# The large low parts of two feed-forward weights in block 0: VectorE subtraction or adding DMA transfer

## The chip, the cores and the metric

The kernel runs on one core of one Trainium2 chip. The metric is the device time of a run in microseconds (us). The median of three runs of the kernel before is 1362.46 us.

## What is computed

The reference is a transformer-like block on one sequence of L = 2048 tokens with D = 576 channels. First comes a state-space convolution (S4D) with layer norm and modulation, then a feed-forward network with F = 4608 hidden units:

```python
x = A_u
mod = (_silu(c) @ w_mod).reshape(c.shape[0], 6, 1, -1)
sa, ca, ga, sb, cb, gb = (mod[:, 0], mod[:, 1], ...)
h = _layernorm(x) * (1 + ca) + sa
x = x + ga * _A_ref(h, ...)          # long convolution by FFT with a kernel made from A, C, dt
h = _layernorm(x) * (1 + cb) + sb
h = jnp.maximum(jnp.einsum("bsd,df->bsf", h, B_w1), 0)
x = x + gb * jnp.einsum("bsf,fd->bsd", h, B_w2)
```

## The kernel before

The 2048 tokens are cut into four blocks of 512. The convolution of block 0 is done ahead. Then the feed-forward network runs through `NB * NF` = 4 x 36 = 144 steps on TensorE; a step is 128 hidden units for the 512 tokens of one block. While the steps of a block run, a generator (`gens[b]`) supplies other work, which the method `step` in `ffn` doles out by a rate per block: in block 0 this is the rest of the convolution kernel (`KGen.rest`: loads of `W2r`, `W` and `Zr` from DRAM, VectorE rotations in lines 464 to 470, matmuls in line 498) and the whole convolution of block 1 (`conv(1)`: loads `Ua`, `Ka`, `R`, VectorE products in lines 1009 to 1015).

A number in float32 is split in two parts that TensorE multiplies in the form fp32r: a high part, which is the number rounded to fp32r, and a low part, which is the number minus its high part. Products of high with high, high with low and low with high are summed. So each step has 14 matmuls of 512 columns for `hps` (line 1309) and 14 for `acc` (line 1335). The hidden units are split by ScalarE and VectorE (`hh`, line 1314, and `hl`, line 1315).

The weights are split in block 0 as they come in, and the low parts are kept in DRAM for blocks 1 to 3. In step g of block 0:

- SyncE (SP) loads `r1` (128 x 640, line 1254, for step g + 3) and `r2` (128 x 576, line 1258, for step g + 2). There are two buffers of each, so that a load waits until the last reader of the buffer two steps back is done.
- ScalarE (ACT) makes the high parts: `hi1`, line 1274 (128 x 640), and `hi2`, line 1284 (128 x 576).
- VectorE (DVE) makes the low parts: `lo1`, line 1279 (128 x 640), and `lo2`, lines 1290 (128 x 64) and 1291 (128 x 512).
- SP writes the low parts to DRAM (`L1d`, `L2d`, line 1390), out of the list `late`, one step after they were made. The weight buffers `w1` and `w2` are three deep.

From block 1 on (g >= 36) the low parts are loaded from `L1d` and `L2d`, and there is no subtraction.

GpSimd (POOL) issues the loads of `KGen.rest` and of `conv` through the software queue (q0); SP's transfers go through the hardware queue (q1). The order on each engine comes from a scheduler, except where an instruction is wrapped in `Kept`, which keeps it in program order with the others so wrapped. For the first three steps the splitting is wrapped, and in the profile its rows stand under line 47, the line of `Kept`. An engine takes its instructions in order, so one that waits holds up all behind it.

Of the kernel before, what the change touches and what calls it, by code (L numbers as in the profile page):

```python
# [10 lines left out]
F32 = mybir.dt.float32  # L11
F32R = mybir.dt.float32r
I32 = mybir.dt.int32
AF = mybir.ActivationFunctionType
ALU = mybir.AluOpType
# [5 lines left out]
D = 576  # L21
# [3 lines left out]
NF = F // P  # L25
# [24 lines left out]
class KGen:  # L50
# [10 lines left out]
    def v(self, out, a, b, op):  # L61
        self.tc.keep_in_program_order(self.nc.vector.tensor_tensor(out, a, b, op=op))  # L62
# [488 lines left out]
class Body:  # L551
# [194 lines left out]
    def main(self, ctx, kg, hooks):  # L746
# [32 lines left out]
        with ExitStack() as c:  # L779
            self.cps = self.pool(c, "cps0", space=PSUM)  # L780
            self.tps = self.pool(c, "tps", space=PSUM)
            self.cv = self.pool(c, "cv0", side="right")
            self.cvl = self.pool(c, "cvl", side="right")
            self.nps, self.ns = 4, 6
            mods, ffn = self.mod_late(), self.ffn(gens)
            self.vec = Kept(tc, nc.vector)
            for w in self.conv(0):
                if w == "mod":
                    next(mods, None)
                elif w in ("weights", "high", "low"):  # L790
                    next(ffn)
                elif w == "rows":
                    hooks[w]()
                elif w in hooks:
                    for _ in hooks[w]:
                        pass
            self.vec = nc.vector
# [444 lines left out]
    def ffn(self, gens):  # L1242

        nc, I, ff = self.nc, self.I, self.ff
        n = NB * NF
        r1, r2, w1, w2 = {}, {}, {}, {}
# [20 lines left out]
        def vec(g):  # L1267
            return (Kept(self.tc, nc.vector) if g < 3 else nc.vector).tensor_tensor

        def copy(g):  # L1270
            return (Kept(self.tc, nc.scalar) if g < 3 else nc.scalar).activation

        def hi1(g):
            copy(g - 1)(w1[g][:, 0], r1[g], AF.Copy)  # L1274

        def lo1(g):
            w, r = w1[g], r1.pop(g)
            if g < NF:
                vec(g)(w[:, 1], r, w[:, 0], op=ALU.subtract)  # L1279
                late.append((self.L1d[g], w[:, 1].rearrange("p k c -> p (k c)")))  # L1280

        def hi2(g):
            w = w2[g] = ff.tile([P, 1152], F32R, tag="w2", bufs=3, name="w2")
            copy(g)(w[:, 0:D], r2[g], AF.Copy)  # L1284

        def lo2(g):
            w, r = w2[g], r2.pop(g)
            if g < NF:
                v = vec(g)
                v(w[:, D:640], r[:, 512:D], w[:, 512:D], op=ALU.subtract)  # L1290
                v(w[:, 640:], r[:, :512], w[:, :512], op=ALU.subtract)
                late.append((self.L2d[g], w[:, D:]))
            else:
                nc.sync.dma_start(out=w[:, D:].bitcast(F32), in_=self.L2d[g % NF])
# [77 lines left out]
        for f in (hi1, hi2):  # L1372
            f(0)
        hi1(1)
        yield
        lo1(0)
        lo2(0)
        lo1(1)
        yield
        load_r2(1)  # L1380
        load_r1(2)
        prev = None
        for g in range(n + 1):
            if g < n:
                if g + 3 < n:
                    load_r1(g + 3)
                if g + 2 < n:
                    load_r2(g + 2)
                for dst, src in late:
                    nc.sync.dma_start(out=dst, in_=src.bitcast(F32))  # L1390
                late.clear()
                new = (g, *first(g))
                if g + 1 < n:
                    hi2(g + 1)
                    lo2(g + 1)
                if g + 2 < n:
                    hi1(g + 2)
                    lo1(g + 2)
                if g + 3 < n:
                    low1(g + 3)  # L1400
                step(g)
            if prev is not None:
                second(*prev)
                if prev[0] % NF == NF - 1:
                    self.evacuate(prev[0] // NF)
            if g < n:
                prev = new
                step(g)
                if g % NF == NF - 1:
                    for _ in gens[g // NF]:  # L1410
                        pass
                    done[0] = 0.0
# [126 lines left out]
```

## Time and profile before

| | |
|---|---|
| median of 3 runs (lowest to highest) | 1362.46 us (1361.05 to 1364.14) |
| the profiled execution | 1357.89 us; its span 1356.1 us |
| mean granted TensorE clock | 0.944 |
| PE busy | 1239.6 us (91%), 10720 matmuls |
| VectorE busy | 891.6 us (66%), 1324 instructions |
| ScalarE busy | 494.9 us (36%), 863 instructions |
| GpSimd busy | 162.6 us (12%), 260 instructions |
| DMA | 345.85 MB, mean 255 GB/s |

Busy times are of the whole span. Block 0 of the feed-forward network runs from about 228 to about 568 us of the span; only there the weights are split. A group's row has the line, the engine, the operation, out<-in, the shapes and the count; behind the first bar stand the busy time in us and the mean duration of one in ns, behind the second the idle time of the engine before it and what ended it. `w` is a buffer of `w1` or `w2`, and `r` one of `r1` or `r2` (the profile leaves buffer numbers out).

### The profile page before, as it was taken

How to read it: one execution, taken by the hardware profiler on the slowest of the kernel's cores; microseconds unless marked ns; L12 is line 12 of the kernel's file. 1: busy time of each engine (PE TensorE's matmuls, PEld its weight loads, DVE VectorE, ACT ScalarE, POOL GpSimd, SP SyncE). 2: the span in 40 equal slices, each digit the busy share in tenths (PEclk: the TensorE clock that was granted, in tenths of full speed). 3: DMA queues.
4: the chain of work that ended last, by engine and by line, in shares of the span. 5: the costliest groups of instructions: out<-in, count | busy, mean ns of one | idle time of the engine just before them, and what ended most of it. 6: DMA issues, size and time to landing. Idle time of an engine off the chain costs nothing.

```text
span 1356.1 us, 26019 instructions
## 1 busy us (share of the span) xinstructions
PE 1239.6 (91%) x10720; PEld 986.5 (73%) x10720; DVE 891.6 (66%) x1324; ACT 494.9 (36%) x863; POOL 162.6 (12%) x260
## 2 busy tenths in 40 slices
PE   4566777899989999999999999999999999999997
PEld 2345555677767687777777887887888888888885
DVE  5889988999955899678556986367997222111112
ACT  5678423222122432622234225433322353233231
POOL 0657511000010100020000000100000000000000
PEclk9558887999978999999999999999999999999998
DMA  8557973776897877798778995777996557666651
GB/s 267 221 223 291 328 271 130 282 249 248 320 332 277 296 248 269 239 382 311 250 246 327 363 371 158 269 230 245 370 387 194 176 175 228 201 195 195 201 184 53
DMA packets 120843, 345.85 MB, mean 255 GB/s; under 512 B 23916, under 2 KB 24212, under 8 KB 109972
## 3 DMA queue, kind: packets, MB, share of 16 engines
q1 hardware_dynamic: 103828, 226.96, 49.7%
q0 software_dynamic: 16384, 115.85, 22.8%
q8 instruction: 84, 1.38, 0.4%
q10 hardware_dynamic: 512, 1.38, 0.3%
q14 instruction: 35, 0.29, 0.1%
HBM read 262.73 MB, written 81.40 MB: 254 GB/s over the span
## 4 chain that ended last, share of the span: by engine, by line
PE 73%; DVE 15%; DMA 5%; issue 4%; ACT 1%; POOL 1%; SPq 0%; ACTq 0%; DVEq 0%; POOLq 0%
PE acc L1335 29%; PE hps L1309 29%; PE kps L498 4%; PE ps_f L829 4%; PE kps L71 2%; PE ph L71 2%; PE ps_i L1036 2%; DVE T L464 1%; DVE W1r L466 1%; DVE T L62 1%; DMA Ua<-Ud 1%; DVE Y L1015 1%; DMA r<-in_w_dram 1%; DMA kd<-ker 1%; DVE W L62 1%
## 5 line engine op out<-in xcount | busy, mean ns | idle before, releaser
L1309 PE MATMUL hps<-xh,w 128*128 128x512 f32 x1152 | 391.3, 400 | 0.7 <-ACT xh L47 0.7
L1335 PE MATMUL acc<-w,hh 128*128 128x512 f32 x1152 | 371.8, 403 | 7.0 <-ACT hh L1314 7.0
L1315 DVE SCALAR_TENSOR_TENSOR hl<-hps,hh 128x512 fp32r<-128x512 f32 x144 | 99.0, 687 | 322.9 <-ACT hh L1314 321.9
L1335 PEld LDWEIGHTS acc<-w,hh 128*128 128x128 f32 x1152 | 217.6, 190 | 55.1 <-ACT hh L1314 8.3
L1309 PEld LDWEIGHTS hps<-xh,w 128*128 128x128 f32 x1152 | 217.3, 190 | 48.5 <-ACT xh L47 1.3
L1309 PE MATMUL hps<-xl,w 128*128 128x512 f32 x576 | 230.7, 401 | 0.2
L1335 PE MATMUL acc<-w,hl 128*128 128x512 f32 x576 | 224.4, 402 | 3.9 <-DVE hl L1315 3.9
L1314 ACT ACTIVATE hh<-hps 128x512 fp32r<-128x512 f32 x144 | 85.9, 597 | 304.0 <-PE hps L1309 302.3
L1284 ACT ACTIVATE w<-r 128x576 fp32r<-128x576 f32 x141 | 96.6, 685 | 236.7 <-PE acc L1335 207.9
L1335 PEld LDWEIGHTS acc<-w,hl 128*128 128x128 f32 x576 | 109.1, 190 | 28.2 <-DVE hl L1315 5.0
L1309 PEld LDWEIGHTS hps<-xl,w 128*128 128x128 f32 x576 | 108.7, 189 | 24.5 <-DVE xl L47 0.8
L1274 ACT ACTIVATE w<-r 128x640 fp32r<-128x640 f32 x140 | 102.6, 733 | 40.6 <-DMA r<-in_w_dram 40.6
L1309 PE MATMUL hps<-xs,w 128*128 128x512 f32 x288 | 97.1, 410 | 0.3 <-DVE w L1279 0.3
L498 PEld LDWEIGHTS kps<-W1r,W2r 128*32 128x32 f32 x3456 | 66.9, 146 | 32.0 <-issue 23.6
L498 PE MATMUL kps<-W1r,W2r 128*32 128x48 f32 (+2 forms) x3456 | 75.9, 238 | 9.2 <-issue 8.2
L71 PE MATMUL kps<-W,W 128*32 128x16 f32 x2304 | 45.1, 218 | 42.7 <-POOL W L68 28.7
L71 PEld LDWEIGHTS kps<-W,W 128*32 128x32 f32 x2304 | 40.4, 150 | 55.0 <-POOL W L68 30.7
L1015 DVE TENSOR_TENSOR Y<-Y,T 128x1152 f32<-128x1152 f32 x60 | 79.4, 1349 | 0.0
L830 ACT ACTIVATE Z<-ps_f 128x288 f32<-128x288 f32 x120 | 48.7, 408 | 68.8 <-PE ps_f L829 67.6
L1453 POOL DMA_DIRECT2D out_dram<-x x16 | 8.7, 544 | 469.0 <-DVE x L1445 466.3
L1309 PEld LDWEIGHTS hps<-xs,w 128*128 128x128 f32 x288 | 53.3, 188 | 12.4 <-DVE w L1279 0.7
L1335 PE MATMUL acc<-hl,w 128*128 128x512 f32 x144 | 57.3, 398 | 0.0
(230 smaller groups left out, 1567.3 us busy)
## 6 DMA issues: line engine op xcount, KB each, us to landing
r<-in_w_dram SPq DMA_DIRECT2D x144, 320.0 KB, 3.5
r<-in_w_dram SPq DMA_DIRECT2D x144, 288.0 KB, 3.7
w<-L1d SPq DMA_DIRECT2D x108, 320.0 KB
w<-L2d SPq DMA_DIRECT2D x108, 288.0 KB, 2.6
W2r<-W2d POOLq DMA_DIRECT2D x18, 1536.0 KB, 8.3
W2d<-W SPq DMA_DIRECT2D x12, 1536.0 KB, 8.6
Ua<-Ud POOLq DMA_DIRECT2D x15, 1152.0 KB, 9.4
W<-W1d POOLq DMA_DIRECT2D x18, 768.0 KB, 10.7
```

The lines of the kernel that those rows point to most:

```text
L62: self.tc.keep_in_program_order(self.nc.vector.tensor_tensor(out, a, b, op=op))
L71: self.tc.keep_in_program_order(self.nc.tensor.matmul(*args, **kw))
L498: nc.tensor.matmul(ps[32 * dd : 32 * dd + 32, q, :], W2[:, r, :, ch], W1[:, :, r, ch], start=(r == 0), stop=(r == 1),)
L829: nc.tensor.matmul(o, fc[:, n2, c, :], src(n2), start=True, stop=True)
L830: ev = nc.scalar.activation(Z[:, n2, c], ps[:, :PC], AF.Copy)
L1015: v(y, y, T, op=op or ALU.add)
L1274: copy(g - 1)(w1[g][:, 0], r1[g], AF.Copy)
L1284: copy(g)(w[:, 0:D], r2[g], AF.Copy)
L1309: nc.tensor.matmul(ps, a, x, start=(i == 0), stop=(i == 13))
L1314: nc.scalar.activation(hh, ps, AF.Relu)
L1315: nc.vector.scalar_tensor_tensor(hl, ps, 0.0, hh, op0=ALU.max, op1=ALU.subtract)
L1335: nc.tensor.matmul(acc[i], a, x, start=(f == 0 and seen[i] == 1), stop=(f == NF - 1 and seen[i] == (3 if i < 4 else 2)),)
```

## The change

In block 0, ScalarE now makes a second, negated copy of the rounded weight in the place of the low part, and a transfer issued by GpSimd adds the unrounded weight onto it: -high + r = low. This replaces the subtraction of 128 x 640 (`lo1`) and the one of 128 x 512 (`lo2`). The small subtraction of 128 x 64 stays on VectorE. The negated copy is the same copy with a scale of -1, and so the negated high part.

```diff
         def hi1(g):
             copy(g - 1)(w1[g][:, 0], r1[g], AF.Copy)
+            if g < NF:
+                copy(g - 1)(w1[g][:, 1], r1[g], AF.Copy, scale=-1.0)
 
         def lo1(g):
             w, r = w1[g], r1.pop(g)
             if g < NF:
-                vec(g)(w[:, 1], r, w[:, 0], op=ALU.subtract)
+                nc.gpsimd.dma_start(
+                    out=w[:, 1].rearrange("p k c -> p (k c)").bitcast(F32),
+                    in_=r.rearrange("p k c -> p (k c)"), accum_op=ALU.add,
+                )
                 late.append((self.L1d[g], w[:, 1].rearrange("p k c -> p (k c)")))
 
         def hi2(g):
             w = w2[g] = ff.tile([P, 1152], F32R, tag="w2", bufs=3, name="w2")
             copy(g)(w[:, 0:D], r2[g], AF.Copy)
+            if g < NF:
+                copy(g)(w[:, 640:], r2[g][:, :512], AF.Copy, scale=-1.0)
 
         def lo2(g):
             w, r = w2[g], r2.pop(g)
             if g < NF:
-                v = vec(g)
-                v(w[:, D:640], r[:, 512:D], w[:, 512:D], op=ALU.subtract)
-                v(w[:, 640:], r[:, :512], w[:, :512], op=ALU.subtract)
+                vec(g)(w[:, D:640], r[:, 512:D], w[:, 512:D], op=ALU.subtract)
+                nc.gpsimd.dma_start(
+                    out=w[:, 640:].bitcast(F32), in_=r[:, 0:512], accum_op=ALU.add
+                )
                 late.append((self.L2d[g], w[:, D:]))
```

The change shifts line numbers: the two adding transfers are lines 1281 and 1297, the negated copies 1276 and 1291, the high part of `w2` is line 1289, `hh` is 1322, the matmuls 1317 and 1343, and the writes to `L1d` and `L2d` line 1398.

The order of the instructions shows three places. The first is GpSimd's queue in the middle of block 0's kernel work (`W2r`, `W`, `Zr` are the loads of three successive pieces of it). Before:

```order
L47 DMA W2r_4_3733<-W2d_4_69 128x3072
L47 DMA W0_6_3735<-W1d_6_83 128x1536
L47 DMA Zr_6_3736<-Zd_6_95 128x192
L47 DMA W2r_5_3947<-W2d_5_70 128x3072
L47 DMA W0_7_3949<-W1d_7_84 128x1536
L47 DMA Zr_7_3950<-Zd_7_96 128x192
```

The same loads after the change:

```order
L47 DMA W2r_4_3754<-W2d_4_69 128x3072
L47 DMA W0_6_3756<-W1d_6_83 128x1536
L1297 DMA w2_3833<-r2_3695 128x512
L47 DMA Zr_6_3757<-Zd_6_95 128x192
L1281 DMA w1_3753<-r1_3693 128x640
L1281 DMA w1_3841<-r1_3807 128x640
L1297 DMA w2_3938<-r2_3809 128x512
L47 DMA W2r_5_3972<-W2d_5_70 128x3072
L47 DMA W0_7_3974<-W1d_7_84 128x1536
L47 DMA Zr_7_3975<-Zd_7_96 128x192
```

Four adding transfers, those of two steps, stand in the queue between one set of loads and the next.

The second is SP's queue at the same stage, with the semaphores that each waits for (DMASW: a transfer of GpSimd's queue has landed; DMAHW: one of SP's). Before:

```order
L1258 DMA r_3249<-in_w_dram 128x576 [waits DMAHW6_49,DVE_49,Activation_49]
L1254 DMA r_3247<-in_w_dram 128x640 [waits DMAHW7_49,DVE_49,Activation_49]
L1390 DMA L2d_167<-w_3195 128x576 [waits DMAHW0_49]
L1390 DMA L1d_132<-w_3098 128x640 [waits DMAHW1_49]
L1258 DMA r_3360<-in_w_dram 128x576 [waits DMAHW2_49,DVE_49,Activation_49]
```

After:

```order
L1254 DMA r_3589<-in_w_dram 128x640 [waits DMAHW2_49,DMAHW4_49,DMASW3_49,Activation_49]
L1398 DMA L1d_135<-w_3405 128x640 [waits DMAHW3_49]
L1258 DMA r_3591<-in_w_dram 128x576 [waits DMASW2_49,DVE_49]
L1398 DMA L2d_170<-w_3536 128x576 [waits DMAHW5_49]
L1254 DMA r_3693<-in_w_dram 128x640 [waits DMAHW6_49,DMASW0_49,Activation_49]
```

A load of a weight waited for VectorE's subtraction, and now waits for the landing of the adding transfer that reads the same buffer.

The third is ScalarE's queue, one step of the same stage. Before:

```order
L1284 ACTIVATE w2_3598<-r2_3463 128x576
L1274 ACTIVATE w1_3527<-r1_3461 128x640
L1314 ACTIVATE hh_3594<-hps_3578 128x512
L508 ACTIVATE ker_0_3115<-kps_3544 128x48x6
L1284 ACTIVATE w2_3726<-r2_3574 128x576
```

After:

```order
L1289 ACTIVATE w2_3397<-r2_3260 128x576
L1291 ACTIVATE w2_3397<-r2_3260 128x512
L1322 ACTIVATE hh_3393<-hps_3377 128x512
L508 ACTIVATE ker_0_3124<-kps_3343 128x48x6
L1289 ACTIVATE w2_3536<-r2_3373 128x576
L1291 ACTIVATE w2_3536<-r2_3373 128x512
L1274 ACTIVATE w1_3405<-r1_3371 128x640
```

Each copy of a weight has a second one behind it, ahead of the next `hh`.

## The prediction

> **What bounds the kernel now.** The change touches block 0 of the feed-forward network alone, so I read the busy times by stretch first: the kernel work (228 to 344 us), its end and the transforms of block 1 (344 to 460), the products of block 1 (460 to 568), all of block 0, and two stretches of later blocks. Behind the busy times stand the granted clock, the DMA share and GB/s.
>
> ```profile
> core 0: us, PE busy (x) PEld busy (x) DVE busy (x) ACT busy (x) POOL busy (x), PEclk, DMA share, GB/s
> 228.00:344.00 116.00, 109.02 (x1304) 85.48 (x1303) 115.27 (x120) 29.57 (x51) 11.48 (x22) 0.97 0.75 270
> 344.00:460.00 116.00, 106.95 (x1657) 83.24 (x1657) 79.06 (x120) 30.45 (x67) 11.48 (x20) 0.91 0.85 302
> 460.00:568.00 108.00, 105.12 (x456) 82.01 (x455) 94.80 (x151) 41.68 (x76) 4.24 (x8) 1.00 0.76 268
> 228.00:568.00 340.00, 321.08 (x3415) 250.73 (x3414) 289.13 (x389) 101.71 (x193) 27.20 (x49) 0.96 0.78 280
> ...
> 750.00:800.00 50.00, 50.00 (x220) 41.09 (x219) 44.57 (x53) 13.39 (x21) 4.25 (x8) 1.00 0.98 372
> ...
> 1200.00:1250.00 50.00, 50.00 (x223) 41.39 (x221) 5.53 (x8) 14.73 (x24) 0.00 (x0) 1.00 0.65 199
> ```
>
> In the first stretch VectorE is busy 115.27 of 116 us: it is the bound there. But the DMA engines are busy 0.75 to 0.85 of the time all through block 0; later they reach 0.98 with TensorE full.
>
> A busy TensorE isn't TensorE at its peak, so I work out its floor. In the last row above it has nothing else to do and runs a 512-column matmul each 50 / 223 = 0.224 us. The rows of the first stretch alone, by line (1309, 1335, then the kernel's 498):
>
> ```profile
> 228.00:344.00 116.00, 44.17 (x170) 30.67 (x168) 0.97 0.75 270
> ...
> 228.00:344.00 116.00, 46.98 (x174) 32.81 (x175) 0.97 0.75 270
> ...
> 228.00:344.00 116.00, 26.34 (x960) 22.39 (x960) 0.97 0.75 270
> ```
>
> 170 + 174 big ones make 77.1 us, with 26.3 us of line 498 the floor is 103.4 of 116 us. So VectorE costs at most 12.6 us here.
>
> The timeline of VectorE shows the same by step (start, duration; the `hl` of one step and that two steps on):
>
> ```profile
> 256.92 0.68 DVE L1315 SCALAR_TENSOR_TENSOR hl<-hps,hh 128x512 fp32r<-128x512 f32 x1
> ...
> 269.88 0.68 DVE L1291 TENSOR_TENSOR w<-r,w 128x512 fp32r<-128x512 f32 x1
> 270.48 0.81 DVE L1279 TENSOR_TENSOR w<-r,w 128x640 fp32r<-128x640 f32 x1
> 271.21 3.42 DVE L466 TENSOR_TENSOR W1r<-W,Zr 128x1536 f32<-128x1536 f32 x2
> ...
> 276.29 0.68 DVE L1315 SCALAR_TENSOR_TENSOR hl<-hps,hh 128x512 fp32r<-128x512 f32 x1
> ```
>
> Two steps take 276.29 - 256.92 = 19.37 us. From start to start the two subtractions that go take 0.60 and 0.73 us.
>
> Last the chain of waits, in whose block 0 stand waits for transfers too; its two longest (start, us):
>
> ```profile
> 280.17 11.73 DMA r<-in_w_dram
> ...
> 512.35 12.85 DMA Ua<-Ud
> ```
>
> One is a weight's load (`r`), the other a load of GpSimd's queue: both kinds get company from the change.
>
> **The change part by part.**
>
> *Removed from VectorE.* 0.60 + 0.73 = 1.33 us in each step. In the first stretch (first two rows) 11 x 0.73 + 10 x 0.60 = 14 us of VectorE's 115 go; it would need 101 us, and TensorE's floor of 103.4 is next. At most 12.6 us are won.
>
> ```profile
> L1279 DVE TENSOR_TENSOR w<-r,w 128x640 fp32r<-128x640 f32 x11 | 9.0, 814 | 0.0
> ...
> L1291 DVE TENSOR_TENSOR w<-r,w 128x512 fp32r<-128x512 f32 x10 | 6.8, 681 | 0.0
> ...
> L1279 DVE TENSOR_TENSOR w<-r,w 128x640 fp32r<-128x640 f32 x11 | 9.0, 815 | 0.0
> ...
> L1291 DVE TENSOR_TENSOR w<-r,w 128x512 fp32r<-128x512 f32 x12 | 8.2, 681 | 0.0
> ```
>
> In the second stretch VectorE is busy 79 of 116 us and isn't last: nothing. In the third (last two rows) it is busy 94.8 of 108 us, and the chain has the transfer of 12.85 us. 11 x 0.73 + 12 x 0.60 make 15 us; I take two thirds, 10 us, an estimate, for VectorE isn't last all the time. The relief is at most 12.6 + 10 = 22 us.
>
> *Added to ScalarE.* Two copies a step. The nearest row is the copy of the high part:
>
> ```profile
> L1274 ACT ACTIVATE w<-r 128x640 fp32r<-128x640 f32 x140 | 102.6, 733 | 40.6 <-DMA r<-in_w_dram 40.6
> ```
>
> At most 2 x 0.73 = 1.46 us a step (one of the two is shorter), some 50 us in block 0, where ScalarE is busy 102 of 340. The cover is its idle time. It isn't perfect: the copies stand ahead of `hh`, and `hh` starts the second half of a step. ScalarE already waits for `r` with `hh` behind it. Cost nothing; without cover 1.46 us a step, about what VectorE gives back.
>
> *Added to GpSimd.* Two issues a step. A plain issue takes 0.54 us by the first row, the dearest in block 0 1.18 by the second; so 37 to 80 us more on an engine busy 27 of 340. The issue time is hidden. The queue is not: an adding transfer waits for ScalarE's copy, and the next `W2r`, `W`, `Zr` stand behind it; the other way round it waits behind a `W2r` that waits for TensorE, or a `Zr` that waits for VectorE.
>
> ```profile
> L1453 POOL DMA_DIRECT2D out_dram<-x x16 | 8.7, 544 | 469.0 <-DVE x L1445 466.3 <-DVE x L1451 2.5
> ...
> L1232 POOL DMA_DIRECT2D kt<-kd x6 | 7.0, 1175 | 60.5 <-PE ps_f L829 58.4 <-DVE W1r L468 2.0
> ```
>
> *Added to the DMA engines: the term that decides.* 320 KB and 256 KB more in each step. The rate at full share is 280 / 0.78 = 359 GB/s (the row of all block 0), so one pass of the bytes takes 0.91 + 0.73 = 1.64 us of all 16 engines. The trace has no adding transfer. It can't take less than about one plain pass; it has to fetch `r` and the destination and write the destination, three movements for a plain transfer's two, so 1.5 passes if fetching and writing count alike, and two if fetching alone sets the pace. I take 1.5 and keep 1 and 2 as the ends. Some 35 steps' weights fall between 228 and 568. Now the engines are busy 0.78 x 340 = 265 us there; 35 x 1.64 = 57 us a pass makes 322, 351 or 380 us for 1, 1.5 or 2 passes. The window of 340 us doesn't hold 351. At 0.95, a little under the 0.98 that the row of 750 to 800 us reaches (block 0's own best stretch has 0.85), the three need 339, 369 and 400 us: no gain, +29, +60.
>
> A page speaks against the change here: the Trainium skill, *Collectives: The Full Stack*, section "The bandwidth ceiling: the fold count and why AG ≠ RS ≠ AR", holds that a reducing transfer runs at half the rate of a copying one, since both operands are fetched through the same reading side. By that rule it is two passes and +60; no run here shows it. Another speaks for it: *DMA: Bandwidth & Descriptors*, section "Where 436 GB/s comes from", gives SBUF to SBUF 435 GB/s where transfers with HBM have some 358. The 359 above agrees with the latter; by the former 1.5 passes would be an estimated 71 us instead of 86, and the sum about +14.
>
> *Moved: when a weight's buffer comes free.* A load of `r` waited for VectorE; now for the landing of the adding transfer, which goes into the same queue as the loads of the kernel work. Landings in the first stretch (count, KB, median us):
>
> ```profile
> W<-W1d POOLq DMA_DIRECT2D x8, 768.0 KB, 10.1
> r<-in_w_dram SPq DMA_DIRECT2D x12, 320.0 KB, 5.4
> ...
> Zr<-Zd POOLq DMA_DIRECT2D x8, 96.0 KB, 7.8
> ```
>
> `Zr` is small and takes 7.8 us because it stands behind `W2r` and `W`. A loop over two steps is then: adding transfer (some 8 to 10 us behind such a burst) + load 5.4 + four copies 2.9 + two issues about 1 = 17 to 19 us. VectorE without the subtractions needs 19.37 - 2.67 = 16.7. So the new loop is about as long as what it replaces, with nothing to spare. Queued behind the waiting load on SP are the other weight's load and both writes to `L1d` and `L2d`.
>
> *Sum.* VectorE's relief of up to 22 us is real but something else is last once it is gone: the DMA engines, at 369 us where block 0 takes 340. That is +29 us against the profiled execution's 1357.89, so about 1387; the median of the runs lies 4.6 above that execution, so 1391 on the median. About 0.2% (2.7 us) is what a measurement can tell from no change here.
>
> **The rivals.**
>
> *The relief pays (faster).* If the adding transfers take a pass or less and the share goes to 0.98 as it did at 750 us, block 0 needs 322 / 0.98 = 329 us: -11. With no loss at all it is -22. For it: the first stretch's VectorE at 99%, and idle DMA between bursts that an adding transfer could fill. It decides when the fetch of the destination costs nothing. 1340 to 1357, about 1351. Chance 0.20.
>
> *Even.* One pass at 0.95: 339 us for 340. 1360 to 1365. Chance 0.06.
>
> *Two passes.* 400 us, +60; with some of it in gaps +45 to +75: about 1422. For it: reading twice is the plain meaning of an add. Against: the 0.78 is a busy share that holds waits as well as bytes. Chance 0.20.
>
> *The buffer's loop.* If landings under the heavier load go to the longest that the chain shows (12.85 for a load of GpSimd's queue, 11.73 for `r`), the loop is 12.9 + 11.7 + 2.9 + 1 = 28.5 us for two steps, 9 over the 19.37, and 17 pairs give some +75 us whatever the bytes cost: about 1437. It decides once the two landings together exceed some 15.5 us. Against: most steps between bursts land sooner (the loads' median is 5.4). Chance 0.10.
>
> That the subtractions are not taken off VectorE is no rival: the order shows the adding transfers in their place.
>
> **How the numbers follow.** Forecast, more work on the DMA engines than block 0 has room for, +3 to +45: chance 0.44. Slower in all 0.44 + 0.20 + 0.10 = 0.74, same 0.06, faster 0.20. The range leaves out the better half of the faster case and the upper part of the two slowest cases, about 0.1 each: 1350 to 1428. The forecast's own range is 1365 to 1408.
>
> **What would show it.** Right: VectorE in block 0 down by some 45 us and no longer full in its first stretch; DMA share of block 0 at 0.9 or more; block 0 some 370 us long; loads of `r` and DMA waits longer in the chain, `hh` late behind a copy that waits for `r`; blocks 1 to 3 unchanged. Wrong: two steps of the first stretch at 17.5 us, near TensorE's floor, with a DMA share under 0.9 (the relief pays), or a step paced by one buffer's loop with a DMA share that hasn't risen.

## The result and the profile after

The kernel after takes 1409.45 us (median of 4 runs, 1401.38 to 1414.38) against 1362.7 us before: the ratio is 1.0338, with a 95% interval of 1.0287 to 1.0388. That is 46.8 us slower. The profiled execution took 1414.38 us with a span of 1412.6 us, at the upper end of its runs, so its loss of 56.5 us in the span is larger than that of the medians.

All of it arises in block 0. By the timeline, the `hl` of step 1 starts 0.9 us later than before, that of step 12 14.1 us later, of step 23 39.3 and of step 36 55.0; from step 40 on the distance is 56.6 to 56.7 us to the end.

The stretches of the kernel after, in the columns of the prediction's first table (block 0 is longer now, so the last row reaches to 615 us; a DMA packet counts whole in the stretch in which it starts, so a share can pass 1):

```profile
228.00:344.00 116.00, 99.74 (x1071) 77.07 (x1071) 92.14 (x89) 37.20 (x65) 30.19 (x42) 0.93 0.97 291
344.00:460.00 116.00, 93.95 (x1771) 75.14 (x1771) 51.88 (x71) 30.79 (x63) 25.22 (x34) 0.90 0.91 283
460.00:568.00 108.00, 96.81 (x365) 71.75 (x364) 71.55 (x105) 44.34 (x84) 25.65 (x34) 0.91 1.03 327
228.00:615.00 387.00, 331.14 (x3378) 255.39 (x3378) 245.84 (x320) 136.64 (x255) 88.73 (x119) 0.92 0.96 292
```

VectorE is no longer full in the first stretch (92.14 of 116 us) and is busy 246 us in block 0 instead of 289. The share of the DMA engines went from 0.78 to 0.96, and neither TensorE nor VectorE fills a stretch. The bound has moved to the DMA engines and to those who wait for them.

The DMA queues and issues of block 0, before (228 to 568 us) and then after (228 to 615 us): packets, MB and share of 16 engines; below, count, KB and median us to landing.

```profile
q1 hardware_dynamic: 21952, 48.44, 40.5%
q0 software_dynamic: 6176, 46.30, 37.3%
...
r<-in_w_dram SPq DMA_DIRECT2D x37, 320.0 KB, 5.2
...
r<-in_w_dram SPq DMA_DIRECT2D x37, 288.0 KB, 2.7
```

```profile
q0 software_dynamic: 16112, 66.62, 62.0%
q1 hardware_dynamic: 20800, 46.02, 33.4%
...
r<-in_w_dram SPq DMA_DIRECT2D x36, 320.0 KB, 4.8
w<-r POOLq DMA_DIRECT2D x34, 320.0 KB, 6.5
...
r<-in_w_dram SPq DMA_DIRECT2D x35, 288.0 KB, 6.7
...
w<-r POOLq DMA_DIRECT2D x35, 256.0 KB, 6.4
```

GpSimd's queue q0 was busy 0.373 x 340 = 127 us and is now busy 0.620 x 387 = 240 us: 113 us more of all 16 engines for 20.3 MB more, 5.57 us a MB. Before, it took 127 / 46.30 = 2.74 us a MB. An adding transfer thus costs 2.03 times what the same queue's plain ones cost per byte. The records of single packets say the same: a packet of 2560 bytes takes 215 ns (median) in an adding transfer and 102 ns in a load or write of SP, and the 69 adding transfers add up to 114 us of the 16 engines.

This alone sets a floor. The engines were busy 265 us in block 0 before; with 114 us more that is 379 us, and a share of 0.96 over the 396 us that block 0 takes in the profiled execution is 380. Even at a share of 1, 379 us are 39 more than the 340 of before, as long as the other transfers take what they took.

The chain of waits at the start of block 0 (start, us):

```profile
235.52 11.06 DMA w<-r
246.70 11.88 DMA r<-in_w_dram
...
270.90 12.51 DMA w<-r
283.47 5.62 DMA r<-in_w_dram
```

An adding transfer lands, and only then does the load into the buffer that it read start. SP's waits show the same. Before, the loads of lines 1254 and 1258 waited for VectorE; after, for the landing (us in total, times, longest):

```profile
SPq L1258 <- DVE w L1291: 169.1, 29, 13.0
...
SPq L1254 <- DVE w L1279: 34.6, 28, 7.6
```

```profile
SPq L1258 <- DMA w<-r: 160.6, 17, 39.8
SPq L1254 <- DMA w<-r: 134.5, 31, 18.1
```

The engines' waits after (us in total, times, longest): ScalarE waits for `r`, and VectorE's `hl` waits for ScalarE's `hh`, which stands behind those copies. `hl <- hh` was 20.8 us in 6 waits in block 0 before. GpSimd waits for the second copy, with the loads of the kernel work behind it.

```profile
POOL w L1297 <- ACT w L1291: 85.0, 15, 13.8
DVE hl L1323 <- ACT hh L1322: 71.6, 18, 11.9
POOL w L1281 <- ACT w L1276: 63.0, 14, 12.0
ACT w L1289 <- DMA r<-in_w_dram: 61.6, 15, 11.8
ACT w L1274 <- DMA r<-in_w_dram: 52.7, 16, 7.1
```

Two other ways to lose time are small in this trace. For loads of GpSimd's queue VectorE waited 18.2 us in all of block 0, and 13.0 us before (4.3 and 2.5 us of it for `Zr`). For an adding transfer to land TensorE waited 3.5 us at most.

So two readings are open. In the first (A), the DMA engines are full, and the bytes set the pace. In the second (B, with its kin C and E), latency does: the round from adding transfer to load to copy, through queues that work in order, whatever the bytes cost. The profile shows signs of both.

### The profile page after: what moved, and what is told of

Read it like the earlier page. It is cut to its first block, busy times and chain, and to the rows that moved or that the text cites. A ratio compares the mean times of both kernels' runs of the same rounds, so it can differ in the third digit from the quotient of the medians.

```text
span 1412.6 us, 26239 instructions
## 1 busy us (share of the span) xinstructions
PE 1258.2 (89%) x10720; PEld 997.7 (71%) x10720; DVE 847.7 (60%) x1252; ACT 535.4 (38%) x935; POOL 225.7 (16%) x332
## 4 chain that ended last, share of the span: by engine, by line
PE 67%; DMA 17%; DVE 6%; issue 5%; ACT 2%; POOL 1%; SPq 0%; POOLq 0%; ACTq 0%; DVEq 0%
PE acc L1343 27%; PE hps L1317 27%; DMA r<-in_w_dram 6%; DMA w<-r 6%; PE ps_f L829 4%; PE kps L498 3%; PE kps L71 2%; PE ph L71 2%; DMA L2d<-w 2%; PE ps_i L1036 2%; DVE T L62 1%; DMA Rd<-K 1%; PE ps_t L1131 1%; POOL W L68 1%; DMA kd<-ker 1%
## 5 line engine op out<-in xcount | busy, mean ns | idle before, releaser
L1343 PE MATMUL acc<-w,hh 128*128 128x512 f32 x1152 | 377.7, 405 | 3.5 <-ACT hh L1322 2.4
L1317 PE MATMUL hps<-xl,w 128*128 128x512 f32 x576 | 235.4, 409 | 0.7 <-DVE xl L47 0.5
L1343 PE MATMUL acc<-w,hl 128*128 128x512 f32 x576 | 232.2, 404 | 1.3 <-DVE hl L1323 1.3
L1343 PEld LDWEIGHTS acc<-w,hl 128*128 128x128 f32 x576 | 110.2, 191 | 25.9 <-DVE hl L1323 2.1
L1036 PE MATMUL ps_i<-V,gc 128*128 128x288 f32 x136 | 43.8, 458 | 19.2 <-DVE x L1041 11.3
```

The lines of the kernel that those rows point to most:

```text
L1036: nc.tensor.matmul(ps[:, :PC], a, b, start=(i == 0), stop=(i == len(ops) - 1))
L1317: nc.tensor.matmul(ps, a, x, start=(i == 0), stop=(i == 13))
L1343: nc.tensor.matmul(acc[i], a, x, start=(f == 0 and seen[i] == 1), stop=(f == NF - 1 and seen[i] == (3 if i < 4 else 2)),)
```

## The experiments

Each run is compared with the kernel before, run beside it on the same chip. Microseconds are differences of the medians.

| run | kernel it starts from | median us | against before | ratio (95% interval) |
|---|---|---|---|---|
| a_plain | after | 1378.22 | +19.2 | 1.0149 (1.0110 to 1.0188) |
| a_half | after | 1394.59 | +35.6 | 1.0257 (1.0231 to 1.0283) |
| a_tiny | after | 1370.97 | +11.9 | 1.0086 (1.0061 to 1.0112) |
| b_bytes | before | 1385.19 | +26.2 | 1.0192 (1.0171 to 1.0212) |
| a_free | after | 1413.03 | +53.0 | 1.0385 (1.0362 to 1.0409) |
| a_plainsp | a_plain | 1399.25 | +39.2 | 1.0285 (1.0251 to 1.0320) |
| b_bytes2 | before | 1361.65 | +1.6 | 1.0010 (0.9994 to 1.0025) |
| b_pool1 | before | 1384.94 | +24.9 | 1.0185 (1.0164 to 1.0206) |
| a_freeL0 | a_free | 1409.35 | +48.2 | 1.0360 (1.0329 to 1.0391) |
| a_L0 | after | 1425.82 | +64.7 | 1.0476 (1.0439 to 1.0514) |
| a_late | after | 1404.59 | +43.4 | 1.0319 (1.0280 to 1.0358) |
| b_part | before | 1369.75 | +10.7 | 1.0061 (1.0036 to 1.0086) |

The scheduler writes the order of the engines anew for each kernel. a_plain has the order of the kernel after on every engine, a_half and a_tiny have the same order as each other, and b_bytes and b_bytes2 have that of the kernel before except on GpSimd. In the others the interleaving moved too, and I read no meaning into differences of some 10 us between them.

**Fewer bytes: a_plain, a_half, a_tiny.** a_plain:

```diff
-                    in_=r.rearrange("p k c -> p (k c)"), accum_op=ALU.add,
+                    in_=r.rearrange("p k c -> p (k c)"),
...
-                    out=w[:, 640:].bitcast(F32), in_=r[:, 0:512], accum_op=ALU.add
+                    out=w[:, 640:].bitcast(F32), in_=r[:, 0:512]
```

> The kernel after, with both adding transfers turned into plain copies of the same tiles, so the low parts in block 0 hold the raw weight instead of the rounding rest (that part of the computation is wrong, nothing else). Issues, queues, copies and waits are the same; only the fetch of the destination goes. Theory A (the DMA engines are full, an adding transfer costs two passes of its bytes): one pass less, 57 us less of all 16 engines' time, so block 0 needs 322 us of transfers and the kernel comes to 1350 to 1370. Theory B (the loop of the two weight buffers through the landing, whatever the bytes cost): the landing stays behind the same bursts on the same queue, and the time stays at 1395 to 1410.

a_half, where the slices are cut to 320 and 256 columns, and a_tiny, where both are cut to 128:

```diff
-                    out=w[:, 1].rearrange("p k c -> p (k c)").bitcast(F32),
-                    in_=r.rearrange("p k c -> p (k c)"), accum_op=ALU.add,
+                    out=w[:, 1].rearrange("p k c -> p (k c)").bitcast(F32)[:, 0:320],
+                    in_=r.rearrange("p k c -> p (k c)")[:, 0:320], accum_op=ALU.add,
```

> The kernel after, with the adding transfers over half of the columns only (320 of 640 and 256 of 512); the other half of the low parts in block 0 keeps the negated high part (wrong there). Same issues, queues, copies and waits, half of the added bytes. Theory A: 57 us less of all 16 engines' time, as with the plain copy of all columns: 1350 to 1370, and the same as that run to about 5 us. Theory B: 1395 to 1410.

> The kernel after, with the adding transfers over 128 columns only (22% of the added bytes); the other columns of the low parts in block 0 keep the negated high part (wrong there). Same issues, queues, copies and waits. Theory A: 25 us of added transfer work fit into block 0, what VectorE gives back shows: 1342 to 1362, at or below the kernel before. Theory B, in its strong form (queue place and round trip, not bytes, set the pace): 1385 or more. The copies or the issues by themselves (ScalarE ahead of hh, GpSimd's order) would show here as a time above 1362 with a DMA share under 0.9.

By the packets' records the transfers in question cost 114 us of the 16 engines after, 64 in a_half, 52 in a_plain and 36 in a_tiny: small packets are dear (65 ns for 512 bytes, 121 for 1280, 215 for 2560). The losses stand in the same order: some 46, 36, 19 and 12 us. In the two pairs of equal order, 62 us less of transfer work (after to a_plain) saves some 27 us, and 27 us less (a_half to a_tiny) saves 24 us. So the size of the transfers counts, against B in its strong form. But a_plain, a_half and a_tiny should have been level with the kernel before by A (265 + 52 = 317, 265 + 64 = 329 and 265 + 36 = 301 us of work in a block 0 of 340 us), and they are not: a_plain and a_tiny lie between what A and B had expected, and a_half, at 1394.59 us, lies at B's lower end. The second stretch (344 to 460 us) of a_plain, a_half and a_tiny, in this order:

```profile
344.00:460.00 116.00, 103.42 (x1686) 81.62 (x1686) 55.34 (x82) 39.27 (x79) 21.05 (x37) 0.94 0.88 323
```

```profile
344.00:460.00 116.00, 90.31 (x1585) 72.67 (x1586) 47.99 (x70) 28.35 (x59) 23.99 (x33) 0.87 0.82 260
```

```profile
344.00:460.00 116.00, 103.27 (x1688) 81.70 (x1687) 57.33 (x82) 37.87 (x77) 28.47 (x38) 0.94 0.87 282
```

Here the engines have room (0.82 to 0.88), TensorE waits all the same, and a_half loses most with the lowest share: a loss that isn't full engines. Of its loss, 21.5 us arise between the `hl` of steps 12 and 14. The chain there (start, us):

```profile
334.13 11.15 DMA w<-r
...
347.55 12.58 DMA L2d<-w
360.17 0.61 ACT w L1291
```

An adding transfer landed late, and behind it a write held up ScalarE's next copy. a_tiny loses 7.6 us in these steps, so they make 13.9 of the 21.4 us that a_half loses more in the profiled executions. So the second pair says little on full engines; the first pair, with shares of 0.96 and 0.90 over block 0, is the better evidence. This also spoils the expectation that a_half and a_plain would be level; they are 16 us apart with 12 us between their transfer work. And a_tiny shows the sign that was named for the copies and issues by themselves, a time above 1362 with a share under 0.9 (1370.97 us; 0.87 from 228 to 615 us). No run has the copies and issues without any transfer, so how much of its 12 us they make is open.

**The bytes alone: b_bytes and b_bytes2.** b_bytes adds to the kernel before, in steps 3 to 12:

```diff
+        def more(g, i):
+            if 3 <= g < 13:
+                nc.gpsimd.dma_start(out=self.scr[:, i], in_=self.x2[0][:, i], accum_op=ALU.add)
```

> The kernel before, with the subtractions still on VectorE, and beside them adding transfers for which nobody waits: in steps 3 to 12 two a step of 576 columns x 128 rows each, from a tile in SBUF onto an idle scratch tile, 5.9 MB in all, the bytes of ten steps of the change. The output is that of the kernel before. Theory A: some 33 us of all 16 engines' time go into the first stretch, whose engines are busy 87 of 116 us; it overflows to 1368 to 1385. Theory B: no weight buffer waits for these landings, so 1360 to 1367.

This run missed its aim. The transfers waited for nothing that comes late, so the scheduler put 19 of the 20 ahead of the kernel work's first loads. GpSimd's timeline (start, duration, in brackets the idle time before it):

```profile
216.71 0.90 POOL L1277 DMA_DIRECT2D scr<-x  x1 [9.02 <-issue]
...
249.96 0.89 POOL L47 DMA_DIRECT2D W<-W1d  x1
```

The first load of `W` goes out at 249.96 us. By the starts of `hl`, the whole loss of the first stretch, 27.2 us, stands at step 1 and stays the same up to step 14. It shows what a queue in order can cost, and nothing on bytes. b_bytes2 reads the finished low part instead, and so takes its place in the right step:

```diff
+                more(g, w[:, 1].rearrange("p k c -> p (k c)")[:, 0:D], 0)
...
+                more(g, w[:, D:], 1)
```

> The kernel before, subtractions still on VectorE, and in steps 3 to 12 two adding transfers a step of 576 columns from the finished low part onto an idle scratch tile, issued on GpSimd's queue behind the subtraction (the earlier try issued them all at once ahead of the kernel work's first loads). Nobody but the next user of the scratch slot waits for them; output as before; the order on all engines but GpSimd is that of the kernel before. 20 transfers x 128 rows x about 0.195 us / 16 engines = 31 us of the engines' time in the first stretch, which has 87 of 116 us taken. Theory A: 118 us of transfers at a share of 0.95 make 124 us, 6 to 12 us slower. Theory B: no weight buffer waits, -2 to +3 us. If over 15 us, the order of GpSimd's queue (kernel work's loads behind transfers that wait for VectorE) is itself a cost.

```profile
228.00:344.00 116.00, 110.15 (x1307) 85.84 (x1308) 114.77 (x121) 29.16 (x49) 29.77 (x42) 1.00 0.98 304
```

The share in the first stretch is 0.98 and the time is that of before: +1.6 us, with 1 in the interval. By the starts of `hl` the distance is 2.0 us at step 0 and 2.0 at step 14. So 32 us of adding transfers (by their packets) took up nearly all of the 29 us that the first stretch had left, at no cost, with no weight's load waiting for them. That is no verdict against A, which becomes a cost only beyond that. It shows that a share of 0.98 over one stretch does no harm by itself; whether it would over all of block 0 was not tried.

**The waits: a_free, a_late, a_L0, a_freeL0.** a_free lets the transfer read the high part, so that `r` is free after ScalarE's copies:

```diff
-                    in_=r.rearrange("p k c -> p (k c)"), accum_op=ALU.add,
+                    in_=w[:, 0].rearrange("p k c -> p (k c)").bitcast(F32), accum_op=ALU.add,
...
-                    out=w[:, 640:].bitcast(F32), in_=r[:, 0:512], accum_op=ALU.add
+                    out=w[:, 640:].bitcast(F32), in_=w[:, 0:512].bitcast(F32), accum_op=ALU.add
```

> The kernel after, with the adding transfers fetching the high part (in the same weight tile) instead of the raw weight r, so that r is free after ScalarE's copies; the low parts in block 0 become zero (wrong there). Same bytes, same sizes of packets, same queue, and the products still wait for the landing; only the raw weight's buffer no longer waits for it. Theory A (full DMA engines): 114 us of added transfer work as in the kernel after, so the loss stays at 40 to 50 us. Theory B (loop of the raw weight's buffers): the loss falls to 20 us or less. If each carries half, some 30.

Nothing was gained. SP's waits in a_free name a reason that would save B:

```profile
SPq L1398 <- DMA w<-w: 134.1, 42, 9.3
```

The loads no longer wait for the landing, but the writes to `L1d` and `L2d` still do, in the same queue ahead of the loads. So theory E: SP's order holds the loads up. Three runs tested it.

a_late issues the writes one step later:

```diff
-                for dst, src in late:
+                for dst, src in late[:-2] if g < NF else late:
                     nc.sync.dma_start(out=dst, in_=src.bitcast(F32))
-                late.clear()
+                late = late[-2:] if g < NF else []
```

> The kernel after, with the writes to L1d and L2d of block 0 issued one step later, when the adding transfer should have landed; the output is that of the kernel after. Loads of r still wait for the landing. Theory A: 40 us slower or more than the kernel before. Theory E: as the run with the high part written, since the wait for r's buffer is left: 30 to 50 us; if the writes were what held SP, under 15 us, and a gain over the kernel after.

a_L0 writes the high part, and a_freeL0 does that and what a_free does, so that neither a load nor a write waits for a landing:

```diff
-                late.append((self.L1d[g], w[:, 1].rearrange("p k c -> p (k c)")))
+                late.append((self.L1d[g], w[:, 0].rearrange("p k c -> p (k c)")))
...
-                late.append((self.L2d[g], w[:, D:]))
+                late.append((self.L2d[g], w[:, 0:D]))
```

> The kernel after, with only the writes to L1d and L2d changed: they write the high part, ready with ScalarE's copy, and not the low part (wrong low parts in blocks 1 to 3). Loads of r still wait for the landing of the adding transfer that reads the same buffer. Same bytes. Theory A: 40 us slower or more. Theory E, if one of the two waits is enough to hold SP (the run that freed r alone gained nothing): 30 to 50 us slower. If the writes were what held SP: under 15 us.

> Both of SP's waits for the landing taken away, all bytes kept: the adding transfers fetch the high part instead of the raw weight (low parts in block 0 become zero), and the writes to L1d and L2d write the high part instead of the low part (wrong low parts in blocks 1 to 3), so that neither a load of r nor a write has to wait for a landing. Same adding transfers, same sizes, same GpSimd queue; the products still wait for the landing. Theory A (full DMA engines): the added 114 us stay, so 40 us slower or more than the kernel before. Theory E (SP's queue in order: loads of r stand behind something that waits for a landing, ScalarE's copies wait for r, hh and the products behind them): within 10 us of the kernel before on either side. Theory F (what is left is the product's own wait for the landing): 20 to 35 us slower.

a_late came out at 43 us, where both theories had it. a_L0 came out at 65, above E's 30 to 50; I have no reason for its being slower than the kernel after, except that its order differs. a_freeL0 is the telling one. Its row of block 0, SP's longest wait, and the loads:

```profile
228.00:615.00 387.00, 329.09 (x3393) 254.19 (x3393) 245.69 (x321) 139.11 (x260) 89.01 (x119) 0.92 0.95 295
```

```profile
SPq L1398 <- ACT w L1289: 159.2, 27, 14.6
```

```profile
r<-in_w_dram SPq DMA_DIRECT2D x36, 320.0 KB, 9.0
...
r<-in_w_dram SPq DMA_DIRECT2D x36, 288.0 KB, 9.8
```

No wait of SP for an adding transfer's landing is left; SP now waits for ScalarE, and ScalarE for the loads themselves, which take 9.0 and 9.8 us (medians) where they took 5.2 and 2.7. TensorE's own wait for the landings is 9.3 us at most (theory F had 20 to 35). The share is 0.95 and the loss 48 us. With the waits for landings gone and the bytes kept the loss is whole: E falls as the main cause, and A, with its floor of 39 us, stands. One reserve: SP's writes now stand in front of the loads and wait for ScalarE's copies, so a round through SP's queue is left in this run too, and no run has the bytes without any such round through all of block 0.

**The queue: a_plainsp.** a_plain's copies issued by SP:

```diff
-                nc.gpsimd.dma_start(
+                nc.sync.dma_start(
```

> The run with plain copies in place of the adding transfers (low parts of block 0 hold the raw weight, wrong there), now issued on SP's queue and not on GpSimd's. Same 52 us of added transfer work; they no longer stand behind the loads of the kernel work (W2r, W: 2.3 MB each time), but SP waits for ScalarE's copy ahead of the next loads. Theory A: as on GpSimd's queue, 14 to 25 us slower than the kernel before. Theory C, that the place in GpSimd's queue is what makes the landing late: a loss of 8 us or less.

Slower by 20 us than on GpSimd's queue: outside what C had (8 us or less), and outside what A had too (14 to 25). ScalarE's wait for `r` grew to 84.3 us, from 49.8 in a_plain: a copy that waits for ScalarE now stands in the queue of the loads. So the run brings a wait of its own and is no clean test of the place behind `W2r` and `W`; but with a share of 0.85 from 228 to 615 us it shows that 39 us can be lost without full engines.

**The relief: b_pool1 and b_part.** b_pool1 moves the first weight's subtraction to GpSimd, without a byte more:

```diff
-                vec(g)(w[:, 1], r, w[:, 0], op=ALU.subtract)
+                (Kept(self.tc, nc.gpsimd) if g < 3 else nc.gpsimd).tensor_tensor(w[:, 1], r, w[:, 0], op=ALU.subtract)
```

> The kernel before, with the first weight's subtraction (128x640) on GpSimd instead of VectorE; nothing else is changed, no bytes are added, the output is right. It asks whether VectorE's relief is worth anything in block 0. If VectorE bounds the first stretch (busy 115 of 116 us): 11 x 0.73 us there and some more in the third stretch, 5 to 12 us faster. If the next limit stands close (loads, TensorE), or GpSimd's subtraction comes late for its reader: same within 3 us or slower.

It gave no relief, and was 25 us slower. The groups of GpSimd and of VectorE in the first stretch of b_pool1, and the same line before:

```profile
L1279 POOL TENSOR_TENSOR w<-r,w 128x640 fp32r<-128x640 f32 x12 | 39.6, 3306 | 19.1 <-ACT w L1274 18.5 <-ACT w L47 0.5
```

```profile
L466 DVE TENSOR_TENSOR W1r<-W,Zr 128x1536 f32<-128x1536 f32 x12 | 24.7, 2093 | 0.0
```

```profile
L466 DVE TENSOR_TENSOR W1r<-W,Zr 128x1536 f32<-128x1536 f32 x12 | 20.5, 1749 | 0.0
```

The subtraction takes 3.31 us on GpSimd in this stretch, and VectorE's own instructions get longer beside it (1749 to 2093 ns); VectorE stays busy 114.78 of 116 us. So the run does not say what relief is worth.

b_part makes the change for the first weight of steps 4 to 12 alone, with the adding transfer of the kernel after:

```diff
+            if 4 <= g < 13:
+                copy(g - 1)(w1[g][:, 1], r1[g], AF.Copy, scale=-1.0)
...
+                if 4 <= g < 13:
+                    nc.gpsimd.dma_start(
+                        out=w[:, 1].rearrange("p k c -> p (k c)").bitcast(F32),
+                        in_=r.rearrange("p k c -> p (k c)"), accum_op=ALU.add,
+                    )
+                else:
+                    vec(g)(w[:, 1], r, w[:, 0], op=ALU.subtract)
```

> The kernel before, with the change made for the first weight of nine steps of the first stretch alone (steps 4 to 12; everything else is subtracted on VectorE as before; the output is right). Nine adding transfers of 320 KB take 9 x 1.79 us = 16 us of the DMA engines (60.9 us for 34 of them in the kernel after), so 103 of 116 us: they fit. VectorE gives back 9 x 0.73 = 6.6 us of 115. Theory A (only bytes beyond what the DMA engines have left cost time): up to 6 us faster by step 12, nothing lost later, so 2 to 6 us faster in all. If the longer way to the low part (ScalarE's copy, GpSimd's issue, the landing behind W2r and W) costs as much as VectorE gives back, as the run with 128 columns suggests: within 2 us, or up to 8 us slower.

It is 0.6% slower (1357.49 to 1374.2 us, a wide spread), where A had 2 to 6 us faster; its median, +10.7, lies above the other reading's "up to 8 us slower" as well. The profiled execution, at 1372.6 us, shows gain and loss apart. By the starts of `hl`, the distance to the kernel before goes from +5.3 us at step 4 to +2.2 at step 9: 0.62 us a step won, nearly the 0.73 that was taken off VectorE. Two jumps take it back, 5.5 us between steps 3 and 4 and 10.5 us between steps 9 and 10. At the first, ScalarE waits 10.3 us for an `r` whose load went out at 259.69 us, 0.35 us after a `W2r` of 1.5 MB. The second one in the chain, and on GpSimd's timeline:

```profile
323.55 11.72 DMA r<-in_w_dram
...
335.97 0.59 ACT hh L1322
```

```profile
323.39 0.54 POOL L47 DMA_DIRECT2D W2r<-W2d  x1 [5.78 <-PE kps L498]
323.92 0.54 POOL L47 DMA_DIRECT2D W<-W1d  x1
```

```profile
SPq L1254 <- DMA w<-r: 63.0, 8, 12.1
```

SP held the load of the first weight back until an adding transfer had landed. The load of the second weight, behind it in SP's queue, so went out at 323.55 us, in the same moment as 2.3 MB for the kernel work, and took 11.72 us; `hh` came 12 us later. The engines' share in this stretch is 0.87. This is what is left when the bytes fit: a load that meets a burst, the second time because a wait in SP's queue moved it there. I take it to be part of the 12 to 19 us of a_tiny and a_plain as well; the chain of a_tiny has the same pairs of landing and load, but it wasn't tested apart there.

No variant beat the kernel before.

## Why the prediction was right, and where its sizes were off

- **VectorE's relief.** Right in the busy time (289 to 246 us in block 0, "some 45 us"), and VectorE is no longer full in its first stretch. "At most 12.6" us there held as a bound: b_part wins 0.62 us a step for 0.73 taken off, five steps long. As a gain it was not reached: a_plain, with both subtractions gone, wins 4.1 us between steps 2 and 11, where 12.6 us over the twelve steps of the stretch would be 9.5 over these nine.
- **ScalarE's copies at nothing.** Their time is as predicted (725 and 617 ns). b_part, with one of the two copies, keeps most of VectorE's relief while they run, so that one costs little; that they stand ahead of `hh` shows in `hl`, which waits 71.6 us for it, because a copy ahead of it waits for `r`. A run with the copies alone is missing.
- **GpSimd's issue.** 0.86 and 0.88 us, between the two rows taken (0.54 and 1.18), and hidden. Of the two fears for its queue, the one for the loads that stand behind the adding transfers came true in a small part (18.2 us of VectorE's waits for them, 13.0 before). The other, that the transfers land late behind `W2r` and `W`, is open: the chain has landings of 11.06 and 12.51 us, but moving plain copies to SP's queue brought a worse wait.
- **The DMA term, "the term that decides".** The mechanism is right: share 0.96, and a loss that stays when the waits for landings are removed. The size was off. The step that failed is "I take 1.5": it is two passes, 114 us for 69 transfers where 86 was taken (57 a pass was worked out; the plain copies of a_plain measured 52). 265 + 114 = 379 us at 0.95 were 399 us, "+60"; the profiled execution lost 56.5 and the medians 46.8. So the 1391 us forecast for the median was 18 us low, and the result lies 1.5 us above the forecast's own range (1365 to 1408), in the rival "two passes" (+45 to +75), which had a chance of 0.20. That it falls into the whole range of 1350 to 1428 says little, for that range reaches from the case in which the relief pays to that of two passes. The argument against that rival, that 0.78 holds waits as well as bytes, did not count for much.
- **The Trainium skill's two pages.** The Trainium skill, *Collectives: The Full Stack*, section "The bandwidth ceiling: the fold count and why AG ≠ RS ≠ AR", states for the ReduceScatter of a collective that both operands are fetched through one reading side, which halves the rate. The trace agrees for the adding transfer of this kernel: 215 ns against 102 for a packet of 2560 bytes. It was the better guide than the half-way value between two ends. The faster rate for SBUF to SBUF, which the Trainium skill has in *DMA: Bandwidth & Descriptors*, section "Where 436 GB/s comes from", does not show here. The plain copies of a_plain take 159 and 196 ns for 4096 and 5120 bytes, on one line with GpSimd's loads from DRAM (178 ns for 4608, 234 for 6144), and in a_plainsp 84 ns for 2048 bytes, on one line with SP's (93 for 2304, 102 for 2560).
- **The ceiling of 0.95.** The kernel after ran at 0.96. b_bytes2 reached 0.98 over 116 us of block 0 at no cost.
- **The buffer's loop.** It was priced as a rival of its own, "whatever the bytes cost". Its sum doesn't come out: 17 pairs of steps at 9 us are 153 us, and "+75" is half of that without a reason given. With few bytes something like it is left (12 us in a_tiny, 11 in b_part), in b_part as single collisions of a load with a burst, and not as a steady loop; with the waits for landings taken away and the bytes kept (a_freeL0) nothing is given back. The two do not simply add up: in a_freeL0 the loads take 9.0 and 9.8 us without the wait, in the kernel after 4.8 and 6.7 with it.
- **The signs.** Block 0 was foreseen some 370 us long and is 396 in the profiled execution. A share over 0.9, longer loads of `r` in the chain and a late `hh` came as said, and blocks 1 to 3 are unchanged.

## What to carry to other kernels

Before an operation is moved from an engine to the DMA engines, count their busy time in the stretch that it runs in, with an adding transfer at two passes of its bytes, and more where rows are short; room on the average is not enough where bursts fill single moments. A transfer in place of an instruction also turns a wait for an engine into a wait for a landing, and what is held up is everything behind it in the waiting queue: here loads that then met a burst. And to decide between full engines and late waits, first add up the engines' work and hold it against the time, for that gives a floor; then keep the bytes and take the waits away, and keep the waits and take the bytes away. Either run alone would have misled here.

## What the runs showed of the hardware that was not expected

- The price of an adding transfer within SBUF grows with a fixed part for each row: 65, 121 and 215 ns for packets of 512, 1280 and 2560 bytes, which is some 27 ns and 0.073 ns a byte. A plain packet on the same queue has some 0.037 ns a byte (178 ns for 4608 bytes and 347 for 9216, before). Adding 22% of the bytes cost 32% of the time (36 of 114 us).
- On GpSimd's queue a plain copy of the same tiles has packets of 4096 and 5120 bytes (159 and 196 ns), the adding one of 2048 and 2560.
- The same subtraction of 128 x 640 takes 0.73 us from start to start on VectorE and 3.31 us on GpSimd in the first stretch of b_pool1 (1.55 to 7.30 us over the run, and GpSimd's durations are rough). VectorE's products of 128 x 1536 (line 466) beside it took 2093 ns instead of 1749.
- TensorE's granted clock was lower where it waited more: 0.82 in the second stretch of a_freeL0 (busy 84.6 of 116 us), 1.00 in the first of b_bytes2 (110.2 of 116). In block 0 it was 0.96 before and 0.92 after; how much of the loss is due to that was not tried.
